# A two-dimensional Fourier transform and a cosine-gated feed-forward layer: queues of three z stores, and 22 pairs of x loads behind the last store

## The chip, the cores and the metric

The kernel runs on one core of one Trainium2 chip. Its engines are TensorE (PE in the profile; PEld is its weight load), VectorE (DVE), ScalarE (ACT), GpSimd (POOL) and SyncE (SP), each with its own list of instructions that it works off in order. DMAs are issued from SP, ACT and POOL and run on 16 DMA engines. The metric is the device time of one execution in microseconds (us).

## The reference

x is 8 batches of 3008 positions by 256 channels, float32.

```python
X = np.fft.fft(np.fft.fft(x, axis=1), axis=2).real     # (8, 3008, 256)
h = X.reshape(24064, 256) @ w_in                       # w_in: 256 x 2048
out = (h * np.cos(h)) @ w_out                          # w_out: 2048 x 256
```

## The kernel before

**Transform.** The 3008 positions are split as 47 x 64, and the input is viewed as `x_r[b, s2, s1, d]` with s1 = 64 consecutive positions. A first half (`first_half`) multiplies folded parts of x by a table of cosines and sines over the 47 values of s2; it works in eight chunks of four values of s1. Its result, a tile `zs` for each chunk, is copied out of PSUM by ScalarE (`take_z`, L398) and stored by `store_z` to two DRAM tensors `zd`: a near part (8 partitions of zs, 16 KB per store) and a far part (40 partitions, 80 KB). `load_z` (L524) reads `zd` back turned, as z, and `second_half` (L538) multiplies z by a second table. The transform over the 256 channels is folded into w_in.

**Layer.** Each batch has six groups of up to 256 transformed positions; a group has eight steps, each over 256 of the 2048 inner columns (`mm1` L722, the cosine on ScalarE and VectorE, `mm2` L813). The loop over all steps is a software pipeline, written out by hand: it runs with manual scheduling, so that each engine's instructions stand in the order in which the code names them. From the dependences between them the recording layer adds the waits on semaphores. DMAs of SP and ACT take eight semaphores in turn, and a DMA also waits until the one before it on its semaphore has landed, where that isn't implied by another wait.

**Opening.** For batch 0, x is loaded by `load_x` (L196) in 14 pieces on SP and ACT into two tiles `xs[0]` and `xs[1]` (shown as xp; 128 partitions by 16 KB each). The side 0 rows of one piece go to partitions 0, 4, 8, ... or 2, 6, ..., the side 1 rows to 1, 5, ... or 66, 70, .... Then the chunks run in the order `order = [1, 0, 2, 3, 4, 5, 7, 6]`, each followed by its near store. These near stores stand on POOL's queue, two for each chunk (e = 0, 1); those of the last chunk in the order, 6, stand on SP and ACT. Behind them SP has the near part of `load_z`, stores of the norm rows (L648), loads of w_out (L248), and then the far stores, all on SP.

**Later batches.** Their x is loaded by SP (L180, batch 1 in part by POOL) into the same two tiles while the layer of the batch before runs; POOL's fold (L337) reads them, for the last time at 1620.0 us.

**End.** The last group's result is combined (`combine_last`), turned on TensorE and stored by `store_last` (L907): four stores on SP, three on ACT, one on POOL. Behind them every engine goes to L1147, the end of the program, where SP waits for the DMAs in flight.

Of the kernel before, what the change touches and what calls it, by code (L numbers as in the profile page):

```python
# [17 lines left out]
SEQ = 3008  # L18
ND = 256
# [115 lines left out]
def kernel(  # L135
# [27 lines left out]
    xs = [spool.tile([128, XP * ND], FP, tag=f"xp{p}", name="xp") for p in range(2)]  # L163
# [98 lines left out]
    sp, act = nc.sync, nc.scalar  # L262
# [228 lines left out]
    order = [DIRECT[0], 0, 2, 3, 4, 5, DIRECT[1], 6]  # L491
# [3 lines left out]
    def store_z(b, c, far):  # L495
        half, q = divmod(c, NCH // 2)
        n = NJ - JA if far else JA
        if (b, far) not in zds:
            zds[b, far] = dpool.tile([128, n * 128], FP, tag=f"zd{far}", bufs=2, name="zd")
        zd = zds[b, far].rearrange("(h e i r) (j d) -> h i (r j) e d", h=2, e=2, r=2, d=128)  # L500
        zs = zss[b, c].rearrange("(e y) (i d) -> y e i d", e=2, d=128)
        y0 = 2 * JA if far else 0
        if b:
            for e in range(2):
                for h in range(2):
                    nc.sync.dma_start(
                        out=zd[h, 2 * c : 2 * c + 2, :, e].rearrange("i y d -> y i d"),
                        in_=zs[y0 : y0 + 2 * n, e, 2 * h : 2 * h + 2],
                    )
            return  # L510
        for e in range(2):
            queue = nc.sync if far else nc.gpsimd
            if c == order[-1] and not far:
                queue = nc.scalar if e else nc.sync
            queue.dma_start(  # L515
                out=zd[half, IP * q : IP * q + IP, :, e].rearrange("i y d -> y i d"),
                in_=zs[y0 : y0 + 2 * n, e],
            )
# [54 lines left out]
    def transform(b):  # L573
        t0 = (b - 1) * NG * 8

        def at(o, *call):
            todo.setdefault(max(t0 + o, LAG - 1), []).append(call)

        for p, o in enumerate((0, 13) if b == 1 else (-20, -9)):
            for k in range(4):  # L580
                at(0 if o == 0 else o + k, load_later_x, b, p, k % 2, k // 2)
        at(4 if b == 1 else -16, load_ends, b)
        for c in range(NCH):
            o = 7 + 8 * (c // 2) + 2 * (c % 2)
            f = o + 2 + c % 2
            for e in range(2):
                aside.setdefault(t0 + o + e, []).append((fold_rows, b, c, e))
                between.setdefault(t0 + o + e + 1, []).append(
                    (fold_cols, xf1[c % 2], xs2[e], e)
                )  # L590
            at(f - 1, clear_spare)
            at(f, first_half, b, c)
            if c % 4 == 0:
                at(f + 1, put_middle, b, c)
            at(f + 1, store_z, b, c, 0)
            at(f + 1, store_z, b, c, 1)
        for e in range(2):
            between.setdefault(t0 + 7 + e, []).append((fold_cols, xfz, xz, e))
        at(38, load_z, b, 0)
        at(38, load_z, b, 1)  # L600
        for g, o in enumerate((42, 44, 46, 49, 52, 55)):
            at(o, second_half, b, g)
# [332 lines left out]
    for b in range(NB):  # L935
        for g in range(NG):
            for fp in range(8):
                s = Step()
# [16 lines left out]
    for c in order:  # L955
        if ahead and c not in DIRECT[1:]:
            chunk(ahead.pop(0))
        first_half(0, c)
        store_z(0, c, 0)
# [41 lines left out]
    n = len(steps)  # L1001
# [62 lines left out]
    for t in range(LAG, n + LAG + 1):  # L1064
# [55 lines left out]
        for call in todo.pop(t, ()):  # L1120
            call[0](*call[1:])


# [1 line left out]
_INS = ['x', 'moe_w_in', 'moe_w_out']  # L1125
# [26 lines left out]
```

## Time and profile before

| | |
|---|---|
| median of 2 runs | 1930.57 us (1928.87 to 1932.28) |
| profiled execution: time, span | 1930.72 us, 1929.0 us |
| TensorE busy | 1913.3 us (99%) |
| VectorE busy | 1784.3 us (93%) |
| ScalarE busy | 1527.6 us (79%) |
| POOL busy | 413.3 us (21%) |
| DMA | 89.16 MB, mean 46 GB/s |
| granted TensorE clock, mean | 0.999 |

The span is the time from the first to the last instruction of the profiled execution; the run's time is 1.7 us more. Shares of busy time are of the span. In the rows that follow, a row of the timeline has the start, the duration, the engine (SPq and ACTq are the queues on which DMAs are issued), the line, the operation, and the tiles as written <- read; the duration of a DMA row is that of its issue, not that of the transfer. A DMA row of digits has the mean busy share of the 16 DMA engines in tenths, in 40 slices of the window.

### The profile page before, as it was taken

Reading aid. Unit: us, or ns where it says so; the run is one execution under the profiler, and the core shown is the slowest. Engines: PE = TensorE matmul, PEld = TensorE weight load, DVE = VectorE, ACT = ScalarE, POOL = GpSimd, SP = SyncE. Lnnn points to the kernel's source line nnn. Section 1 sums busy time; section 2 is a strip of 40 time slices with the busy share of each in tenths; the row PEclk is TensorE's granted clock in tenths of the full one; section 3 lists DMA queues with packets and bytes.
Section 4 is the critical chain, followed back from the end, with each engine's and each line's share of the span. In section 5 each row is a group of like instructions: output and inputs, shape, how many; then the busy total and the mean of one; then the engine's idle time right before and its main releaser. Section 6 shows DMA issues by size and latency. Waiting matters only on the chain.

```text
span 1929.0 us, 30474 instructions
## 1 busy us (share of the span) xinstructions
PE 1913.3 (99%) x9502; PEld 1685.2 (87%) x9502; DVE 1784.3 (93%) x3340; ACT 1527.6 (79%) x2870; POOL 413.3 (21%) x501
## 2 busy tenths in 40 slices
PE   8999999999999999999999999999999999999998
PEld 5888899888998889888898888988889888898887
DVE  7999989999899998999989999999999999999998
ACT  4788888888787887878878887788877888788775
POOL 4322112221122211222112221122211222111111
PEclk9999999999999999999999999999999999999999
DMA  7311210012111121112211022100131000210000
GB/s 218 97 49 47 75 52 26 24 46 77 43 26 28 48 81 34 28 25 57 79 29 30 21 57 83 30 25 25 54 85 31 24 20 24 55 28 10 12 22 23
DMA packets 160729, 89.16 MB, mean 46 GB/s; under 512 B 108664, under 2 KB 155375, under 8 KB 158227
## 3 DMA queue, kind: packets, MB, share of 16 engines
q1 hardware_dynamic: 157727, 84.25, 16.1%
q10 hardware_dynamic: 1752, 1.77, 0.3%
q8 instruction: 76, 1.25, 0.3%
q0 software_dynamic: 1088, 1.19, 0.2%
q14 instruction: 86, 0.70, 0.1%
HBM read 49.88 MB, written 37.28 MB: 45 GB/s over the span
## 4 chain that ended last, share of the span: by engine, by line
PE 96%; DMA 2%; DVE 1%; POOL 0%; SPq 0%; issue 0%; ACT 0%; ACTq 0%; DVEq 0%; POOLq 0%
PE M L813 58%; PE H L722 34%; PE pb L538 2%; PE pz L431 2%; DMA w<-in_moe_w_out_dram 1%; DMA xp<-in_x_dram 1%; DMA xs<-in_moe_w_in_dram 0%; POOL VX L865 0%; DMA zd<-zs 0%; PE pz L362 0%; SPq L515 0%; PE M L431 0%; DMA xz<-in_x_dram 0%; PE pz L419 0%; DVE xp L210 0%
## 5 line engine op out<-in xcount | busy, mean ns | idle before, releaser
L813 PE MATMUL M<-S,VX 128*128 128x256 f32 (+1 forms) x2304 | 612.4, 375 | 0.0
L813 PEld LDWEIGHTS M<-S,VX 128*128 128x128 f32 x2304 | 437.8, 190 | 49.9
L753 ACT ACTIVATE r<-H 128x512 f32<-128x512 f32 (+1 forms) x384 | 226.0, 589 | 263.3 <-DVE h L738 262.2
L763 ACT ACTIVATE r<-r 128x1024 f32<-128x1024 f32 (+1 forms) x384 | 394.7, 1028 | 21.9 <-DVE r L757 17.3
L722 PE MATMUL H<-pq,WC 128*128 128x256 f32 (+1 forms) x1536 | 393.6, 379 | 0.7 <-ACT H L692 0.7
L722 PE MATMUL H<-pq,WS 128*128 128x256 f32 (+1 forms) x1536 | 388.0, 375 | 0.9 <-ACT ew L733 0.9
L813 PE MATMUL M<-r,w 128*128 128x256 f32 (+1 forms) x1536 | 387.9, 375 | 0.4 <-DVE r L767 0.4
L692 ACT ACTIVATE H<-nb,wn 128x256 f32<-128x256 f32 (+1 forms) x762 | 360.6, 473 | 15.4 <-DMA wn<-wd 1.5
L738 DVE TENSOR_TENSOR h<-ew,H 128x512 f32<-128x512 f32 (+1 forms) x384 | 259.4, 676 | 100.2 <-PE H L722 64.1
L722 PEld LDWEIGHTS H<-pq,WC 128*128 128x128 f32 x1536 | 283.4, 190 | 49.9 <-ACT r L753 16.2
L813 PEld LDWEIGHTS M<-r,w 128*128 128x128 f32 x1536 | 300.2, 196 | 28.0 <-DVE r L767 0.7
L722 PEld LDWEIGHTS H<-pq,WS 128*128 128x128 f32 x1536 | 291.4, 190 | 35.1 <-ACT ew L733 2.0
L757 DVE SCALAR_TENSOR_TENSOR r<-r,H 128x512 f32<-128x512 f32 (+1 forms) x384 | 258.9, 674 | 25.1 <-ACT r L753 9.1
L865 POOL TENSOR_TENSOR cb<-cb,mr 128x256 f32<-128x256 f32 (+3 forms) x190 | 159.5, 850 | 522.6 <-DVE S L788 486.4
L733 ACT ACTIVATE ew<-H 128x512 f32<-128x512 f32 (+1 forms) x384 | 225.7, 588 | 54.2 <-PE H L722 45.7
L778 DVE TENSOR_TENSOR S<-r 128x512 f32<-128x512 f32 (+1 forms) x384 | 259.7, 676 | 0.1
L757 DVE SCALAR_TENSOR_TENSOR r<-r,h 128x512 f32<-128x512 f32 (+1 forms) x384 | 259.5, 676 | 0.0
L767 DVE SCALAR_TENSOR_TENSOR r<-h,r 128x512 f32<-128x512 f32 (+1 forms) x384 | 258.3, 673 | 0.0
L767 DVE SCALAR_TENSOR_TENSOR r<-H,r 128x512 f32<-128x512 f32 (+1 forms) x384 | 256.8, 669 | 1.0 <-ACT r L763 0.3
L753 ACT ACTIVATE r<-h 128x512 f32<-128x512 f32 (+1 forms) x384 | 236.0, 614 | 0.0
L813 PE MATMUL M<-S,w 128*128 128x256 f32 (+1 forms) x768 | 226.1, 376 | 1.3 <-DVE S L788 1.3
L337 POOL TENSOR_TENSOR xs<-xp 113x512 f32<-113x512 f32 x112 | 142.9, 1276 | 388.5 <-DVE S L788 388.5
(106 smaller groups left out, 1585.3 us busy)
## 6 DMA issues: line engine op xcount, KB each, us to landing
out_dram<-ob SPq DMA_DIRECT2D x726, 32.0 KB
xp<-in_x_dram SPq DMA_DIRECT2D x256, 56.0 KB
z<-zd SPq DMA_DIRECT2D x8, 1280.0 KB
zd<-zs SPq DMA_DIRECT2D x224, 40.0 KB
nb<-nd SPq DMA_DIRECT2D x39, 128.0 KB
zd<-zs SPq DMA_DIRECT2D x224, 8.0 KB
xp<-in_x_dram SPq DMA_DIRECT2D x52, 48.0 KB
xp<-in_x_dram SPq DMA_DIRECT2D x42, 49.0 KB
```

What stands on the lines that cost most here:

```text
L337: return nc.gpsimd.tensor_tensor(out=xs2[e][0:XL], in0=xv[:, 0], in1=xv[:, 1], op=ALU.subtract if e else ALU.add,)
L692: nc.scalar.activation(out=s.H[:, u * T : u * T + T], in_=s.nb[:, 0:T], func=AF.Copy, bias=0.25, scale=wn[:, f : f + 1],)
L722: nc.tensor.matmul(s.H[:, u * T : u * T + T], lhsT=W[:, 128 * f : 128 * f + 128], rhs=s.pq[:, e * T : e * T + T], start=False, stop=True, ...
L733: nc.scalar.mul(out=s.ew[:, 0 : 2 * s.T], in_=s.H[:, 0 : 2 * s.T], mul=2.0)
L738: return nc.vector.tensor_tensor(out=s.h[:, 0 : 2 * T].rearrange("p (u t) -> p u t", u=2)[:, :, ::-1], in0=s.ew[:, 0 : 2 * T].rearrange("p ...
L753: nc.scalar.activation(out=r, in_=h, func=AF.Copy, bias=BIG, scale=1.0)
L757: nc.vector.scalar_tensor_tensor(out=r, in0=r, scalar=-BIG, in1=h, op0=ALU.add, op1=ALU.subtract)
L763: nc.scalar.activation(out=r, in_=r, func=AF.Sin, bias=0.0, scale=SIN_SCALE)
L767: nc.vector.scalar_tensor_tensor(out=r, in0=h, scalar=-0.25, in1=r, op0=ALU.add, op1=ALU.mult)
L778: return nc.vector.tensor_tensor(out=sv[:, 0:2], in0=gv[:, 2:3].to_broadcast([128, 2, T]), in1=gv[:, 0:4:3], op=ALU.subtract,)
L813: nc.tensor.matmul(acc[key][m // 2][:, 256 * (m % 2) : 256 * (m % 2) + T], lhsT=w, rhs=a, start=first, stop=s.fp == 7, skip_group_check=True,)
L865: return nc.gpsimd.tensor_tensor(out=o, in0=a, in1=b, op=ALU.subtract if less else ALU.add)
```

## The change

The near stores of chunks 5 and 7, the two before the last in the order, now take the same queues as those of chunk 6: e = 0 on SP, e = 1 on ACT. And behind everything else, `store_last` included, 22 pairs of loads are appended. A pair's two loads read the same kind of piece of x: k rows that lie 64 positions apart, n positions of 1 KB from each. They write it to k partitions of xs[0] and xs[1], each k partitions from p0 in steps of a gap; the first load of a pair takes one tile, the second the other, in turn. The first is always on SP, the second on SP or ACT. No instruction reads what they bring, and the output is computed as before.

```diff
--- before.py
+++ after.py
@@ -510,7 +510,7 @@
             return
         for e in range(2):
             queue = nc.sync if far else nc.gpsimd
-            if c == order[-1] and not far:
+            if c in order[5:] and not far:
                 queue = nc.scalar if e else nc.sync
             queue.dma_start(
                 out=zd[half, IP * q : IP * q + IP, :, e].rearrange("i y d -> y i d"),
@@ -1120,6 +1120,42 @@
         for call in todo.pop(t, ()):
             call[0](*call[1:])
 
+    x_flat = x.rearrange("b s d -> (b s) d")
+    probes = (
+        (16, 16, 2, 4, 2, 4, sp),
+        (16, 16, 32, 4, 32, 4, sp),
+        (16, 16, 0, 8, 0, 8, sp),
+        (16, 16, 0, 7, 0, 7, sp),
+        (16, 16, 64, 4, 64, 4, sp),
+        (16, 16, 32, 2, 32, 2, sp),
+        (16, 16, 0, 6, 0, 6, sp),
+        (16, 16, 2, 4, 66, 4, act),
+        (16, 16, 34, 4, 35, 4, act),
+        (16, 16, 2, 8, 6, 8, act),
+        (32, 16, 32, 2, 32, 2, sp),
+        (32, 16, 0, 4, 0, 4, sp),
+        (32, 16, 0, 4, 1, 4, sp),
+        (32, 16, 0, 4, 1, 4, act),
+        (32, 16, 0, 2, 0, 2, sp),
+        (32, 16, 0, 3, 0, 3, sp),
+        (32, 16, 32, 3, 32, 3, sp),
+        (32, 8, 0, 3, 1, 3, sp),
+        (32, 8, 0, 4, 1, 4, sp),
+        (48, 10, 0, 2, 1, 2, sp),
+        (48, 10, 32, 2, 33, 2, sp),
+        (48, 10, 0, 2, 33, 2, act),
+    )
+    for m, (k, n, pa, sa, pb, sb, queue) in enumerate(probes):
+        for j, (p0, gap, by) in enumerate(((pa, sa, sp), (pb, sb, queue))):
+            src = x_flat[SEQ : SEQ + 64 * k].rearrange("(r i) d -> r i d", i=64)
+            by.dma_start(
+                out=xs[(m + j) % 2][p0 : p0 + gap * (k - 1) + 1 : gap, 0 : ND * n].rearrange(
+                    "r (i d) -> r i d", d=ND
+                ),
+                in_=src[:, 16 * j : 16 * j + n],
+                max_dma_last_dim=1024,
+            )
+
```

## The prediction

> **What bounds the kernel now.** I read the page's first three parts, then the chain that ended last, then the two ends of the span: the opening, where the stores move, and the last microseconds, where the loads are added.
>
> ```profile
> span 1929.0 us, 30474 instructions
> PE 1913.3 (99%) x9502; PEld 1685.2 (87%) x9502; DVE 1784.3 (93%) x3340; ACT 1527.6 (79%) x2870; POOL 413.3 (21%) x501
> ...
> PE 96%; DMA 2%; DVE 1%; POOL 0%; SPq 0%; issue 0%; ACT 0%; ACTq 0%; DVEq 0%; POOLq 0%
> ```
>
> TensorE holds 96% of the chain; DMA holds 2%, nearly all of it in the opening. Bytes are no bound: 46 GB/s in the mean. So a transfer costs time only where TensorE isn't running beside it. The timeline of SP's queue shows where SP stands when the kernel ends, and the DMA row of a window from 1923 to 1929 us (40 slices of 0.15 us) when its last bytes land:
>
> ```profile
> 1919.67 3.50 SPq L925 DMA_DIRECT2D out_dram<-ob  x6
> 1923.90 2.62 SPq L907 DMA_DIRECT2D out_dram<-ob  x4
> ```
> ```profile
> DMA  2233333333332168999084488757881000000000
> ```
>
> SP issues its last store until 1923.90 + 2.62 = 1926.5 us. The last bytes move at slice 31, 1927.6 us; the span ends at 1929.0. Between 1926.5 and the end no compute engine has work. Whatever is appended behind L907 lies on the path in full.
>
> **The appended loads: how many bytes.** One load is k rows of n x 1 KB. Twenty have 16 rows of 16 KB (256 KB each, 5.24 MB). The other 24 have 32 or 48 rows: 14 of 512 KB, 4 of 256 KB, 6 of 480 KB, 11.34 MB. Together 44 loads, 16.58 MB. The order of the built program puts 39 on SP behind its four L907 stores and 5 on ScalarE behind its last two. Nothing reads what they bring; but SP at L1147 waits for outstanding DMAs before the end, so the kernel waits for the last one.
>
> **How fast the bytes move.** The opening loads x in the same form: rows of one sequence position every 64 KB, packets of 1 KB, 32 or 16 partitions. Two windows with all DMA engines busy give the rates, the first (5 to 11 us) mostly 32-row loads, the second (11 to 12.5 us) mostly the 16-row load of rows 31 to 46, which ScalarE issues at 7.83:
>
> ```profile
> DMA packets 2091, 1.96 MB, mean 327 GB/s; under 512 B 174, under 2 KB 2091, under 8 KB 2091
> ```
> ```profile
> DMA packets 367, 0.35 MB, mean 232 GB/s; under 512 B 27, under 2 KB 367, under 8 KB 367
> ```
>
> So the 16-row loads take 5.24 MB / 232 = 22.6 us, the others 11.34 / 327 = 34.7, together 57.3 us of transfer. The bounds: all at 327 is 50.7 us, all at 232 is 71.5.
>
> [...]
>
> **How often the DMA engines stand empty.** The loads alternate between two buffers so that the first load of a pair always writes the buffer that the second load of the pair before wrote. Where their rows meet, the first must wait until that load has landed, and SP, which issues in order, stands with nothing behind it in flight. The built order names these waits, by rows that really coincide and not by ranges. Going through the list, the rows meet at pairs 2, 3, 4, 6, 7, 8, 10, 11, 12, 15 and 18 (counted from 0): 11 times. Elsewhere (rows 2, 6, .. 62 against 32, 36, .. 92, say) another load is still in flight.
>
> The price of one standstill is read from the only larger load that ran with nothing beside it, the first z load, 256 KB:
>
> ```profile
> 25.39 0.35 SPq L524 DMA_DIRECT2D z<-zd  x1
> ```
> ```profile
> 28.03 1.13 PE L538 MATMUL pb<-BJ,z 128*128 128x128 f32 x8 [1.65 <-DMA z<-zd]
> ```
>
> From issue to the matmul that waits for it are 2.64 us. Its packets run from about 26.3 to 27.4; 0.92 us lie before them and 0.63 behind, 1.55 us in which no byte moves. The bounds: the 1 KB store of a norm row at 107.57, which SP waits for, lets the next issue go at 108.66, 1.09 us; the quickest x load on POOL's queue (56 KB) lands after 2.8 us, about 2.7 without its bytes. I take 1.55, the row nearest in size and kind. Issue itself is covered: L196's 256 KB issues took 0.62 us each, less than the 0.80 us that 256 KB moves in.
>
> **The sum behind the last store.** 0.92 (first packets) + 57.3 (transfer) + 11 x 1.55 = 17.1 (standstills) + 0.63 (last landing) = 75.9 us. SP begins at 1926.6 (the wait for the buffers themselves is over: their last reader, L337, ran at 1620). Behind the last landing comes what now lies behind the output's: bytes end 1927.6, landing 0.63, so about 0.8 to the end. New span 1926.6 + 75.9 + 0.8 = 2003.3. The old output's tail lies under the first load's start. The profiled execution took 1930.72 for a span of 1929.0, 1.7 more: **2005.0 us**, 74 us or 3.9% over its own 1930.72 and over the median 1930.57, which is the same.
>
> **The moved z stores.** Four near stores (chunks 5 and 7) leave POOL's queue, which issues them from 21.31 on at 0.54 us each; two go to SP, two to ScalarE. ScalarE issues one in 0.53 us (row at 21.73); it stands idle 1.24 us before the next copy and 0.6 before L627, so that at most 0.2 us slips. On SP they stand in the idle stretch 15.83 to 21.72, but their bytes queue behind 512 KB of input weights that run to 24.0. The z load at 25.39 waits for them all and can come at most 0.9 us earlier. That would shorten TensorE's wait of 1.65 us, but not the path: the chain in this stretch goes over the weights (to 24.45), the norm row's copy at 25.88 and the load of w_out (27.32, 5.02 us). I take 0, bounds -0.9 and +1.
>
> **The rivals.**
> - *The row pattern is free and standstills are short:* 0.92 + 50.7 + 11 x 1.09 + 0.63 = 64.2 us, 1993. For it: in the opening, stretches with 16-row loads in flight also ran above 300 GB/s. Against: 11 to 12.5 us.
> - *Slower all over:* uneven rows pull the 32- and 48-row loads to 232 GB/s too (71.5 + 18.7 = 90 us, 2019), or standstills cost 2.7 (88.6 us, 2018). For it: in the opening two queues kept the engines fed; here it is nearly SP alone. Against: 29 to 30 us, where SP alone moved 1 KB packets at 364 GB/s.
> - *Each load waits for the one before:* 44 x 1.55 + 57.3 = 125.5 us, 2055. Against: the waits in the built order.
> - *Not slower:* the loads run beside TensorE. The buffers are free from 1621, and the page's DMA slices there are 0 to 2 tenths; if SP reached the loads 77 us before its last store, by 1850, they would cost nothing and the time would stay at 1930.7. It decides by SP's place in its list alone, and there they stand behind L907. The like holds if a load whose buffer nobody reads were dropped or not awaited; the built order has all 44, and SP's waits between them would keep all but the last landing.
>
> **How the numbers follow.** Forecast (1997 to 2015) 0.61, pattern free 0.17, slower all over 0.15, one by one 0.03, not slower or dropped 0.04. From 1990 to 2026 the range takes in the whole of the first rival's price and both forms of the second; what it leaves out is the last two and the rarer sums of two bounds. A measurement here can tell about 2%, 38.6 us, from no change; even all bytes at 364 GB/s with no standstill is 47 us. So slower by over 2% has 0.96, within 2% 0.03, faster 0.01.
>
> **What would show it.** L1151 issues on SP from 1926.6 to about 2000; about 57 us of full DMA slices cut by 11 gaps of about 1.5 us; about 220 GB/s mean over the tail; TensorE's last matmul still at 1924.5; the z load at 24.5 to 25.4. A first TensorE idle longer than now in the opening, or L1151 rows before 1926, would prove me wrong, as would gaps or rates outside the bounds above.

## The result, and the profile after

The changed kernel takes 2021.76 us (median of 2 runs, 2020.40 to 2023.11) against 1930.57: the ratio is 1.0472, 95% interval 1.0455 to 1.049. It is 91 us slower. Forecast were 2005.0 us, 74 more than before, with a range of 1990 to 2026.

The profiled execution took 2023.11 us for a span of 2021.3. The page's first lines and the chain's shares:

```profile
span 2021.3 us, 30537 instructions
...
PE 1913.8 (95%) x9502; PEld 1686.8 (83%) x9502; DVE 1784.2 (88%) x3340; ACT 1527.7 (76%) x2870; POOL 411.0 (20%) x497
...
PE 92%; DMA 2%; DVE 1%; SPq 0%; issue 0%; ACT 0%; POOL 0%; ACTq 0%; DVEq 0%; POOLq 0%
```

TensorE is busy for 1913.8 us, 0.5 more than before: nothing in the computation is slower. Its share falls because the span is longer. The timeline of SP's queue and TensorE's last row in the timeline say where the span grew:

```profile
1923.26 2.63 SPq L907 DMA_DIRECT2D out_dram<-ob  x4
1925.99 85.83 SPq L1151 DMA_DIRECT2D xp<-in_x_dram  x39
```
```profile
1923.20 0.66 PE L895 MATMUL po<-ident,cb 128*128 128x128 f32 x4 [0.27 <-POOL cb L865]
```

Before, that last row was:

```profile
1923.83 0.65 PE L895 MATMUL po<-ident,cb 128*128 128x128 f32 x4 [0.28 <-POOL cb L865]
```

The last matmul ends at 1923.9 us (before: 1924.5), SP begins with the loads at 1926.0 and issues until 2011.8. Everything behind 1926 is the loads and their bytes. SP's own waits give the same picture (engine, line, what it waited for: us in total, times, longest):

```profile
SPq L1151 <- DMA xp<-in_x_dram: 60.2, 18, 6.4
...
SPq L1183 <- DMA xp<-in_x_dram: 8.1, 3, 5.1
```

For 60 of the 86 us SP stands between two loads waiting for an earlier one; the 8.1 us at L1183 are the last loads landing. How the DMA engines fare meanwhile is seen best in a short window, 1931 to 1941 us in slices of 0.25 us: busy tenths, then GB/s, then the sum.

```profile
DMA  9940000000595999999600000000013699999840
GB/s 381 361 148 0 0 0 0 0 0 0 53 111 172 365 336 299 254 217 168 111 12 0 0 0 0 0 0 0 0 41 70 156 303 340 316 344 287 152 86 4
DMA packets 1325, 1.27 MB, mean 127 GB/s; under 512 B 84, under 2 KB 1325, under 8 KB 1325
```

These are the end of pair 1 and all of pairs 2 and 3 (pairs are counted from 0). Ahead of pairs 2 and 3 stands an empty stretch, as the prediction said. The two are seven and nine empty slices wide, 1.75 and 2.25 us, and the load behind one starts slowly: 53, 111, 172 GB/s before it runs.

### The profile page after: what moved, and what is told of

Read it like the earlier page. It is cut to its first block, busy times and chain, and to the rows that moved or that the text cites. A ratio compares the mean times of both kernels' runs of the same rounds, so it can differ in the third digit from the quotient of the medians.

```text
span 2021.3 us, 30537 instructions
## 1 busy us (share of the span) xinstructions
PE 1913.8 (95%) x9502; PEld 1686.8 (83%) x9502; DVE 1784.2 (88%) x3340; ACT 1527.7 (76%) x2870; POOL 411.0 (20%) x497
## 4 chain that ended last, share of the span: by engine, by line
PE 92%; DMA 2%; DVE 1%; SPq 0%; issue 0%; ACT 0%; POOL 0%; ACTq 0%; DVEq 0%; POOLq 0%
PE M L813 55%; PE H L722 32%; PE pb L538 2%; PE pz L431 1%; DMA xp<-in_x_dram 1%; DMA wn<-wd 0%; DMA zd<-zs 0%; DMA w<-in_moe_w_out_dram 0%; PE pz L465 0%; SPq L515 0%; PE pz L362 0%; PE M L431 0%; PE pz L419 0%; DVE r L767 0%; DVE S L778 0%
## 5 line engine op out<-in xcount | busy, mean ns | idle before, releaser
L813 PE MATMUL M<-r,VX 128*128 128x256 f32 (+1 forms) x768 | 225.2, 375 | 0.0
```

What stands on the lines that cost most here:

```text
L813: nc.tensor.matmul(acc[key][m // 2][:, 256 * (m % 2) : 256 * (m % 2) + T], lhsT=w, rhs=a, start=first, stop=s.fp == 7, skip_group_check=True,)
```

## The experiments

### The two parts apart

The near stores alone, four of them, two of each chunk:

```diff
 # before.py, store_z
-            if c == order[-1] and not far:
+            if c in order[5:] and not far:
```

> Only the near stores of chunks 5 and 7 move; no load is appended. Theory (their bytes queue behind the input weights, and the path of the opening goes over the weights): 0 against before, at most 0.9 us faster, at most 1 us slower; the z load is issued some 0.4 us earlier relative to the first x load's landing. Rival (the moved stores shorten the path): about 1 us faster, 0.05%.

Measured: 1931.47 us against 1929.71, ratio 1.0003, interval 0.9994 to 1.0012. The medians differ by 1.8 us, but both kernels' times scatter from 1928.5 to 1932.4, and the ratio over all of them shows no difference. The interval reaches 1.2 us to the faster side and 2.3 to the slower, so that a gain or a loss of 1 us isn't ruled out. The z load is at 23.66 us in the profiled execution of this run, 25.39 before. The next run, in which the stores stay where they were, has it at 24.80, so that part of such a difference is scatter between executions; how much the stores bring isn't shown.

The loads alone:

```diff
 # after.py, store_z
-            if c in order[5:] and not far:
+            if c == order[-1] and not far:
```

> Only the 44 loads are appended; the near stores stay where they were. Theory (all of the 91 us come from the tail): 2020 to 2024 us, +91 against before. Rival (a part of it comes from the moved stores): less than +89.

Measured: 2023.35 us (2019.75 to 2023.86), ratio 1.0477, interval 1.0461 to 1.0493. That is +93.6 us; the intervals of this ratio and of the change's 1.0472 overlap. No part of the change's cost is seen outside the tail.

### The loads beside TensorE

```diff
+    def load_pair(m): ...            # the two loads of pair m, both on SP
+    for m in range(len(probes)):
+        todo.setdefault(n - 40 + m, []).append((load_pair, m))
```

> The same 22 pairs of loads, all on SP, one pair per step of the pipeline from step 344 on (about 1738 us) instead of behind the last store; the moved near stores stay moved. Theory (they cost what they cost because no engine works beside them): within 3 us of before, TensorE's last matmul within 2 us of where it is. Rival (SP's order or the DMA engines' load delays the output stores between them, and through the two output tiles VectorE and TensorE): 10 us or more over before.

Measured: 1930.04 us against 1929.71, ratio 1.0001, interval 0.9992 to 1.001. No difference is seen: the same bytes, all on SP and one pair per step of the pipeline, cost nothing there. SP waits for earlier loads here too, 42.4 us in 15 waits against 60.2 in 18 above, but TensorE doesn't stand for it. The stretches of this run around them (length; busy time of PE, PEld, DVE, ACT, POOL; granted clock; DMA share; GB/s):

```profile
1640.00:1738.00 98.00, 98.00 (x499) 91.30 (x499) 89.92 (x170) 78.60 (x143) 9.91 (x14) 1.00 0.21 55
1738.00:1850.00 112.00, 112.00 (x520) 99.46 (x519) 107.58 (x196) 88.50 (x153) 14.07 (x18) 1.00 0.61 151
1850.00:1925.00 75.00, 71.29 (x331) 62.40 (x330) 68.14 (x126) 50.72 (x87) 13.16 (x17) 1.00 0.08 19
```

With DMA at 151 GB/s, TensorE is busy for 112 of 112 us. The mechanism of the prediction's rival "not slower" is real; it wanted only the other place.

### Standstills or rate?

The prediction was 17 us short. Two terms of the sum can hold that: the standstills, or the rate of the transfers. The first experiment takes the standstills away and keeps the rest.

```diff
+    bufs = (xs[0], xs[1], VX, w2)
-                out=xs[(m + j) % 2][p0 : p0 + gap * (k - 1) + 1 : gap, 0 : ND * n].rearrange(
+                out=bufs[(2 * m + j) % 4][p0 : p0 + gap * (k - 1) + 1 : gap, 0 : ND * n].rearrange(
```

> As the changed kernel, but the loads go over four buffers in turn (both x tiles, and the two tiles of w_out's sums and of w_out, which nothing reads any more by then), so that a load meets the rows of one that is four or so behind it. Bytes, row patterns and queues stay. Theory (standstills cost about 21 us of the changed kernel's tail and the row patterns set the rate of the rest, 227 GB/s in the mean): about 2002 us, the loads' stretch some 75 us without gaps. Rival (each standstill also slows the load that follows it, a ramp of a microsecond or so; without standstills the bytes move at 327 GB/s as in the opening): 1981 to 1985 us. Rival (standstills are free, the rate is all): 2020 us.

Measured: 2001.14 us, ratio 1.0366, interval 1.0352 to 1.038. That is 22.2 us less than the loads alone in the same comparison, **2.0 us for each of the 11 waits that the prediction counted**, and 71 us remain. The rival of free standstills, 2020, falls. The DMA row of this kernel from 1929 to 1997.5 us:

```profile
DMA packets 16896, 16.58 MB, mean 242 GB/s; under 512 B 704, under 2 KB 16896, under 8 KB 16896
```

All 16.58 MB move in 68.5 us at 242 GB/s. The engines are busy nearly throughout; one empty stretch of 1.1 us is left, at 1953.5, where pair 10 begins. Up to there, with the 16-row loads and one of 512 KB, the rate is 236 GB/s; from 1954.5 to 1997.5, with all others, it is 252. The rival with 327 GB/s behind the standstills falls. In a window of the same run, 1927 to 1990 us, the GB/s row shows where the rate changes:

```profile
GB/s 203 132 244 295 254 214 221 219 218 207 226 297 216 194 218 356 155 26 283 238 237 335 355 385 386 292 209 203 183 214 226 230 267 263 250 243 212 279 231 255
```

Only the four slices at 335 to 386, 1960 to 1966 us, are fast throughout. By the order of the list and the times of issue (1954.48 to 1962.08) they are the pairs with 32 rows in steps of 4, partitions 0, 4, .. and 1, 5, ... That is the pattern of the opening's 32-row loads, from which the prediction had its 327.

### The rate by row pattern

The kernel before, and behind its last store eleven groups of eight loads of 256 KB:

```diff
+    groups = ((16, 16, 2, 4, 4), (16, 16, 32, 4, 4), (16, 16, 0, 8, 4), (32, 8, 0, 4, 4),
+              (32, 8, 0, 2, 4), (32, 8, 32, 2, 4), (32, 8, 0, 3, 4), (32, 8, 0, 1, 4),
+              (128, 2, 0, 1, 4), (16, 16, 32, 4, 1), (128, 2, 0, 1, 1))
+    for k, n, p0, gap, turns in groups:
+        for m in range(8):
+            ...                      # on SP; to bufs[m % turns][p0 :: gap], k rows of n KB
```

> The kernel before, with eleven groups of eight 256 KB loads of x behind the last store, all on SP, source rows 64 positions apart and packets of 1 KB as in the change. Nine groups go over four buffers in turn: 16 rows at 2, 6, ..; 16 at 32, 36, ..; 16 at 0, 8, ..; 32 rows at 0, 4, ..; 32 at 0, 2, ..; 32 at 32, 34, ..; 32 at 0, 3, ..; 32 at 0, 1, ..; 128 at 0, 1, ... The last two write one buffer, each load over the one before: 16 rows at 32, 36, .. and 128 rows. [...] Rival (one queue alone can't feed 1 KB packets): no group over 260. The two chained groups: the standstill is the time between two issues less 256 KB at the group's rate; theory 2.0 to 2.2 us for the 16 rows as in the changed kernel, and 1.55 for the 128 rows if the form of a load sets it, the same 2.0 to 2.2 if not.

This kernel ran once. One stretch within each of the first nine groups (no compute engine works there; the last three numbers are the granted TensorE clock, the DMA share and GB/s):

```profile
1928.00:1937.00 9.00, 0.00 (x0) 0.00 (x0) 0.00 (x0) 0.00 (x0) 0.00 (x0) 0.50 1.12 203
1938.00:1944.50 6.50, 0.00 (x0) 0.00 (x0) 0.00 (x0) 0.00 (x0) 0.00 (x0) 0.50 0.95 299
1946.00:1955.00 9.00, 0.00 (x0) 0.00 (x0) 0.00 (x0) 0.00 (x0) 0.00 (x0) 0.50 1.08 192
1958.50:1963.50 5.00, 0.00 (x0) 0.00 (x0) 0.00 (x0) 0.00 (x0) 0.00 (x0) 0.50 0.86 261
1965.50:1973.50 8.00, 0.00 (x0) 0.00 (x0) 0.00 (x0) 0.00 (x0) 0.00 (x0) 0.50 1.12 202
1974.00:1982.00 8.00, 0.00 (x0) 0.00 (x0) 0.00 (x0) 0.00 (x0) 0.00 (x0) 0.50 0.99 253
1982.50:1989.50 7.00, 0.00 (x0) 0.00 (x0) 0.00 (x0) 0.00 (x0) 0.00 (x0) 0.50 1.04 268
1990.00:2000.00 10.00, 0.00 (x0) 0.00 (x0) 0.00 (x0) 0.00 (x0) 0.00 (x0) 0.50 1.13 205
2001.00:2006.50 5.50, 0.00 (x0) 0.00 (x0) 0.00 (x0) 0.00 (x0) 0.00 (x0) 0.50 0.99 326
```

| group | partitions | GB/s |
|---|---|---|
| 16 rows | 2, 6, .. 62 | 203 |
| 16 rows | 32, 36, .. 92 | 299 |
| 16 rows | 0, 8, .. 120 | 192 |
| 32 rows | 0, 4, .. 124 | 261 |
| 32 rows | 0, 2, .. 62 | 202 |
| 32 rows | 32, 34, .. 94 | 253 |
| 32 rows | 0, 3, .. 93 | 268 |
| 32 rows | 0, 1, .. 31 | 205 |
| 128 rows | 0, 1, .. 127 | 326 |

The number of rows isn't it: 16 rows run at 192, 203 and 299, 32 rows at 202 to 268. Nor does one queue hold 1 KB packets to 260 GB/s: four groups are over it, the fastest at 326, all from SP alone. Four groups stand at 192 to 205, five at 253 to 326. Three of the four have their rows within partitions 0 to 63; the fourth, 0, 8, .. 120, spans all partitions. Why it runs with the other three isn't shown.

Among the five the rates differ: 253, 261, 268, 299 and 326. The 261 is in part an effect of the stretch chosen, which begins with 0.75 us at 8 to 164 GB/s; from 1959.25 to 1963.5 the group runs at 290. What keeps it there isn't shown.

The DMA share misleads here. The four groups at 192 to 205 GB/s show 1.08 to 1.13, the other five 0.86 to 1.04, so that a high share doesn't say that many bytes move. What the engines do in that time isn't shown.

To see the row pattern decide a whole kernel, first all loads in steps of 4, same bytes, over the four buffers:

```diff
-        (16, 16, 2, 4, 2, 4, sp),
+        (32, 8, 0, 4, 1, 4, sp),
         ...                          # 256 KB: 32 x 8 KB, 512: 32 x 16, 480: 32 x 15; queues kept
```

> As the four buffers, with the same bytes in each load and the same queues, but all loads with 32 rows at partitions 0, 4, .. or 1, 5, ..: 256 KB as 32 rows of 8 KB, 480 KB as 32 rows of 15 KB. Theory (the row patterns alone keep the transfers from the opening's rate): the loads' stretch falls to 16.58 MB / 350 GB/s = 47 us and 2 at its ends, 1975 to 1982 us in all. Rival (the rate is that of one queue, or of many loads in flight): 1995 us or more, as with four buffers.

Measured: 1983.98 us, ratio 1.0287, interval 1.027 to 1.0304. By the ratios that is 15 us less than with the mixed patterns, by the medians 17. It is 2 us over the range that the theory gave, and 11 under the rival's 1995. The DMA rows from 1928 to 1981 us:

```profile
GB/s 204 320 290 286 236 244 227 274 273 335 188 296 260 340 201 235 380 257 339 362 386 373 367 383 360 385 380 386 369 383 382 315 184 349 250 304 356 385 380 286
DMA packets 16886, 16.58 MB, mean 313 GB/s; under 512 B 702, under 2 KB 16886, under 8 KB 16886
```

From 1953 to 1969 us, where 512 KB loads move, the rate is 360 to 386 GB/s throughout, 377 in the mean. From 1928 to 1953, mostly 256 KB loads with the same partitions, the mean is 272. So the pattern isn't all.

Then one number changed, the step:

```diff
-        (32, 8, 0, 4, 1, 4, sp),
+        (32, 8, 0, 2, 1, 2, sp),
         ...
```

> As the run with all loads at partitions 0, 4, .. or 1, 5, .. over four buffers, but with the 32 rows at 0, 2, .. or 1, 3, .., partitions 0 to 63 alone. One size is changed, the step. [...] Rival (the number of rows or the wait for the load four behind sets the rate): 1984 us, no change.

Measured: 2011.23 us, ratio 1.0424, interval 1.0406 to 1.0441, 26 to 27 us more for the same loads, so that the rival's 1984 falls. At the 202 GB/s of the pattern run's group at 0, 2, .. 62, an estimate, 16.58 MB take 82 us; from 1928 to 2007 us the bytes moved at 207 GB/s:

```profile
DMA packets 16648, 16.34 MB, mean 207 GB/s; under 512 B 697, under 2 KB 16648, under 8 KB 16648
```

### What a standstill costs

All loads in steps of 4 again, but over the change's two buffers, so that the first load of every pair but pair 0 writes over the load just before it.

```diff
-                out=bufs[(2 * m + j) % 4][...]
+                out=xs[(m + j) % 2][...]          # and all rows at 0, 4, ..
```

> All loads with 32 rows at partitions 0, 4, .., but over the two buffers of the change: now the first load of every pair writes over the one just before it, 21 standstills in place of none. Theory (a standstill costs 2.0 to 2.2 us, the empty time and the slow first load behind it): 1984 + 21 x 2.1 = 2026 to 2031 us. Rival (1.55 us, as in the prediction): 2016 us or less.

Measured: 2028.51 us, ratio 1.0509, interval 1.0494 to 1.0525. That is 43 us by the ratios, 44.5 by the medians, over the four buffers for 21 such waits, **2.0 to 2.1 us** each. The prediction's 1.55 would have given 2016.

The price is a mean, and only part of it is empty time. The packets of this run leave 18 empty stretches of 0.9 us or more, 28 us in all: mostly 1.7 us, four of 1.0 to 1.2 around the loads on ScalarE's queue, and none of that length at the other three waits, which stand next to such loads too. The rest, some 15 us, is lost while bytes move, at a lower rate than with four buffers.

The last two groups of the pattern run take one standstill apart. In 2033 to 2043 us each load of 128 rows waits for the one before (slices of 0.25 us):

```profile
DMA  0000676961000007579500000026696100000477
GB/s 0 0 0 0 98 102 217 344 242 45 0 0 0 0 4 152 90 250 389 172 25 0 0 0 0 0 74 156 193 324 238 66 0 0 0 0 0 123 139 229
```

Such a load comes every 2.67 us: SP issues at 2033.07 and 2035.74. Four to six of some eleven slices are empty; for about 1.4 us, six or seven slices with their ends, the load moves, though 256 KB would need 0.8 at 327 GB/s: alone, the first one starts at 98 to 102 GB/s, a third of that rate. The 16 rows of 16 KB come every 3.09 us (2008.43 and 2011.52). Less the bytes at each group's own rate (0.88 us at 299 GB/s, 0.80 at 326), a wait costs 2.2 us with the 16 rows and 1.9 with the 128. So the form of a load makes 0.3 us between these two groups, and the 1.9 lies between the 1.55 and the 2.0 that had been expected. In both, some 0.5 us of it is the slow start and end of the load, which no empty slice shows.

## Why the prediction was right, and where it was off

**The direction and the place** were right, by the reason given: SP reaches the loads only behind its last store, no engine works beside them, and L1183 waits for the last. The loads beside TensorE cost 0.3 us, not told from nothing, the same loads behind the end 93.6. One sign named for being wrong, L1151 before 1926, is met by 0.01 us (1925.99); it says nothing against the place, since in this execution the last matmul too ends 0.6 us earlier than before. SP issues until 2011.8, not 2000, and the tail's mean from 1926 to 2020 is 179 GB/s, not 220: both follow from the two terms below.

**The moved stores** at 0: the ratio 1.0003 fits, though its interval is wider than the bounds -0.9 and +1. The reason given fits less well. The z load is at 24.37 in the profiled run of the changed kernel, 1.0 us earlier and just outside the 24.5 to 25.4 of the prediction, and TensorE waits 1.71 us for it, not less than the 1.65 before. And the chain in the opening goes another way than the step had it:

```profile
22.75 1.42 DMA zd<-zs
...
24.37 0.35 SPq L524
...
25.42 0.40 SPq L248
...
25.87 5.76 DMA w<-in_moe_w_out_dram
```

A z store and the issue of the z load now lie on the path, since the load of w_out stands behind them on SP. That nothing came of it in the time is measured; that the path would go over the weights was not so in this execution.

**How many standstills:** the count of eleven waits for the load just before is right, and the price from eleven (2.0) agrees with that from 21 (2.0 to 2.1). That the trace also shows eleven empty stretches of 0.7 us or more is luck. Their sum is 19.0 us. Eight are whole, 1.7 to 2.3 us, at pairs 2, 3, 4, 6, 11, 12, 15 and 18. The stretches at pairs 7 and 10 are 1.1 and 0.8 us. Pair 8 leaves none: its second load, issued early on ScalarE's queue, moves while the first waits. And one of 0.8 us stands where nothing was foreseen, ahead of pair 14's second load, which waits for pair 13's first.

**The price of a standstill** was too small: 1.55, measured 2.0 to 2.1, so 17.1 us in the sum should have been 22. The row was well chosen, the z load's 2.64 us from issue to use; a 256 KB load of 128 rows in a chain takes 2.67. But the whole empty stretches are longer than 1.55, and the step charged every load at a steady rate: at 327 GB/s, 0.8 us for 256 KB, behind five of the eleven, at 232 behind the other six. The z load's own 1.1 us of transfer, 238 GB/s with nothing beside it, already showed a lone load moving at less than 327.

**The rate** was the larger miss. The step "how fast the bytes move" gave the 32- and 48-row loads 327 GB/s because the opening's 32-row loads had it. The 16-row loads came out as forecast in the mean, 232 GB/s against a measured 236 in the run with four buffers. That is partly luck, since three of their patterns alone ran at 192, 203 and 299. The others moved at 252 there. What carried over was the step of 4 over all partitions, not the number of rows; only 8 of the 24 loads have that step, the six of 512 KB in pairs 11 to 13 and the two of 256 KB in pair 18, and the stretch of the former on SP ran at 335 to 386 with four buffers. Measured there: 242 GB/s in the mean, 68.5 us in place of 57.3, 11 us more.

Mended by these two terms, 11.2 and 5.1, the sum is 2021.3; measured were 2021.76. That agreement proves little, since both terms were taken from runs of these same loads. The price of a wait is borne out by loads of another pattern, the mean rate isn't. Both misses went the same way, and it was the width of the range, not the forecast, that held the result. What happened is the first form of the rival "slower all over" (32- and 48-row loads at 232 too: 71.5 us of transfer, 2019), which had 0.15, and a part of its second. The forecast's own range, 1997 to 2015, missed.

Why the five faster groups of the pattern run, at 253 to 326 GB/s, stay under the 360 to 386 of the 512 KB loads in steps of 4 is open. With four buffers pair 10, 512 KB loads with rows at 32, 34, .. 94, moves at 237 to 283 GB/s in the three slices ahead of the fast four, and the pairs behind it, in steps of 4, at 335 to 386. The size of a load matters too: in the run with all loads in steps of 4 the mean was 377 GB/s where 512 KB loads moved and 272 where mostly 256 KB ones did. How the rows of one load fall on the DMA engines wasn't tried.

## What to carry to other kernels

Behind the last store the loads cost their whole time, 93.6 us by themselves, and some 22 us of it were waits: two buffers whose rows meet left eleven empty stretches, about 2 us for each wait, where four buffers left one of 1.1 us. The same transfers beside a busy TensorE made no difference that shows (ratio 1.0001), so look first for a place and only then at the transfer. In these runs the rate went with the partitions and with the size of a load: in steps of 4 over all 128 partitions the loads ran at 313 GB/s in the mean, those of 512 KB at 377, and within 0 to 63 the same loads at 207.

## What had not been expected of the hardware

- In the pattern run's last group a load with nothing beside it moved 256 KB in about 1.4 us, not 0.8, even with 128 rows: the first one started at some 100 GB/s for half a microsecond.
- The DMA engines showed a share of 1.13 while they moved 205 GB/s, and 0.95 while they moved 299.
- 16 rows at 32, 36, .. 92 ran at 299 GB/s, 16 rows at 0, 8, .. 120 at 192: spreading the rows wider made them slower.
